# Batch 0's v issued by SyncE, q and k issued first by GpSimd

## The chip, the cores and the metric

The kernel runs on one core of a Trainium2 chip. The metric is device time in microseconds. Three runs of the kernel before took 262.04, 263.99 and 264.71 us; their median is 263.99.

## The reference

Sparse attention over 4 batches, 8 heads, 768 positions and a head size of 64, followed by a gated feed-forward layer over all 3072 tokens:

```python
k_sum = k.reshape(B, H, nb, block, D).max(axis=3)      # block = 32, nb = 24
v_sum = v.reshape(B, H, nb, block, D).mean(axis=3)
scores_l = scale * q @ k.T      # kept where |i - j| < 16, otherwise -1e9
scores_s = scale * q @ k_sum.T + log(block)
a = softmax(concat(scores_l, scores_s))
attn = a @ concat(v, v_sum)
h = x @ w_in                    # x: attn with the heads side by side, 3072 x 512
out = (h * clip(h + 3, 0, 6) / 6) @ w_out
```

Inputs and output are float32. The kernel computes in bfloat16 on the matrix engine.

## The kernel before

The heads are taken in pairs: p = 0 to 3, two heads of 64 making 128 partitions. For each batch and pair the kernel brings q and k into transposed form (`Tq`, `K`), computes the local scores in blocks of 64 keys by 94 queries (`Sl`), the scores against the block maxima (`Ss`), and the weighted sum with its denominator (`AV`). The result, for half a batch at a time (384 tokens, eight such tiles), goes through the first projection (`F1`, w_in) and the second (`F2`, w_out).

Batch 0 has its own beginning. Its v is read in float32 into the tile `vf` by `load_vf(p)`, with two transfers of 192 KB per pair, one per head: partition k holds row k of each of the 12 key blocks, so each piece that is contiguous in memory is a row of 64 numbers, 256 bytes. From `vf` come two things. `vcast` (L247) casts it into the block-diagonal bfloat16 tile `vbd`. `vsum0` (L256) sums blocks of 32 rows with four matmuls per pair; every second pair the sums are copied out and moved into the layout of `vst` by a small transfer that SyncE issues (L263). The loads of q and k (`load_q`, `load_k`) cast from float32 to bfloat16 on the way. They take pair 0, pair 1, and pairs 2 and 3 together; of q only the first 480 rows come at first, and the other 288 rows of all pairs later, with one transfer (L432).

All loads before the change are issued by GpSimd (queue POOL), in the order in which they are written. Between them GpSimd makes the constants: `ident` for transposing (L155 to 158), the local `mask` (L165 to 172) and `hm4` for the block sums (L180 to 186). Behind them come four loads for each of w_in and w_out. At most eight of POOL's transfers are under way in the trace before its next one waits for an old one to land. `pace` (L519) holds the loads of batch 1 back until the first projection of tile 0 has come to its twelfth slice.

For the start PE, ACT and DVE, too, run in the order in which the code is written, and it is this order that decides who waits for v:

```python
    v_first(0)          # vcast(0), vsum0(0)
    zero_rest()
    v_first(1)
    K(0, 0)
    Tq(0, 0, 0)
    v_first(2)
    S_first(0)
    v_first(3)
    K(0, 1)
    Tq(0, 1, 0)
    S_first(1)
```

Then follow `K(0, 2)`, `Tq(0, 2, 0)`, the first `Ss` and `AV`, pair 3, and the rest of the first half's `AV`. The first projection of tile 0 needs the `AV` of all four pairs. After the start a plan of slots (`at_slot`) places the work of attention between the projections' matmuls.

Transposition is by TensorE for batches below NPE, which is 4 (L25), and by a transposing transfer (`X`) otherwise; with four batches `X` is never reached.

Of the kernel before, what the change touches and what calls it, by code (L numbers as in the profile page):

```python
# [32 lines left out]
def kernel(  # L33
# [9 lines left out]
    nc = tc.nc  # L43
    B, H, S, _ = q.shape
    NP = H // 2
# [36 lines left out]
    kb_t, qb_t, vr_t, vf = {}, {}, {}, {}  # L82

    def load_k(b, p, n=1):

        if b < NLONG:
            t = ld.tile([RP, 2 * n, RUN, D], BF16, tag=f"kb{n}", name="kb", bufs=2)
            nc.gpsimd.dma_start(out=t[:], in_=k[b, 2 * p:2 * p + 2 * n].rearrange("h (p s) d -> p h s d", s=RUN))
        else:
            t = ld.tile([128, NT, 2, D], BF16, tag="kb", name="kb")  # L90
            load_natural(t, k, b, p)
        for i in range(n):
            kb_t[b, p + i] = t, i

    def load_q(b, p, n=1, part=None):

        if b < NLONG:
            lo, hi, r = cut(part)
            t = ld.tile([(hi - lo) // r, 2 * n, r, D], BF16, tag=f"qb{n}", name="qb", bufs=1 if n == 4 else 2)
            nc.gpsimd.dma_start(  # L100
                out=t[:], in_=q[b, 2 * p:2 * p + 2 * n, lo:hi].rearrange("h (p s) d -> p h s d", s=r))
        else:
            t = ld.tile([128, NT, 2, D], BF16, tag="qb", name="qb")
            load_natural(t, q, b, p)
        for i in range(n):
            qb_t[b, p + i, part] = t, i

    def cut(part):
        return {None: (0, S, RUN), 0: (0, QCUT, RUN), 1: (QCUT, S, RUN)}[part]

    def load_natural(t, src, b, p):
        for j in range(2):
            nc.gpsimd.dma_start(out=t[:, :, j], in_=src[b, 2 * p + j].rearrange("(s p) d -> p s d", p=128))  # L113
# [9 lines left out]
    def load_vf(p):  # L123

        if not vf:
            t = gp.tile([128, NP, NK, D], F32, tag="g", name="vf")
            vf.update({i: t[:, i] for i in range(NP)})
        for j in range(2):
            nc.gpsimd.dma_start(out=vf[p][64 * j:64 * j + 64],  # L129
                                in_=v[0, 2 * p + j].rearrange("(n k) d -> k n d", k=KB))  # L130

    def load_vrows(b, g):
# [9 lines left out]
    def load_w_in(c):  # L142
        w = d_ff // 4
        nc.gpsimd.dma_start(out=w_in_sb[:, :, c * w:(c + 1) * w], in_=w_in_v[:, :, c * w:(c + 1) * w])

    def load_w_out(c):
# [4 lines left out]
    ctx.enter_context(tc.manual_schedule(engines={ET.Pool}))  # L151
    start = tc.manual_schedule(engines={ET.PE, ET.Activation, ET.DVE})
    start.__enter__()
    load_vf(0)
    ident = const.tile([128, 128], BF16, tag="id", name="ident")  # L155
    nc.gpsimd.memset(ident[:], 1.0)
    nc.gpsimd.affine_select(out=ident[:], in_=ident[:], compare_op=ALU.is_equal, fill=0.0, base=0,
                            channel_multiplier=1, pattern=[[-1, 128]])
    load_vf(1)
    load_k(0, 0)  # L160
    load_q(0, 0, 1, 0)
    load_vf(2)


    mask = const.tile([128, WIN], BF16, tag="mask", name="mask")  # L165
    nc.gpsimd.memset(mask[:], 1.0)
    for j in range(2):
# [2 lines left out]
                                channel_multiplier=-1, pattern=[[1, WIN]])  # L170
        nc.gpsimd.affine_select(out=m, in_=m, compare_op=ALU.is_ge, fill=0.0, base=2 * HALO,
                                channel_multiplier=1, pattern=[[-1, WIN]])
    load_vf(3)
    load_k(0, 1)
    load_q(0, 1, 1, 0)
    load_k(0, 2, 2)
    load_q(0, 2, 2, 0)


    hm4 = const.tile([RS, 4, D], F32, tag="hm4", name="hm4")  # L180
# [30 lines left out]
    for p in range(2, NP):  # L211
        zero_off_diagonal(nc.vector, vbd[p])
    NK0 = 7
    load_w_in(0)

    def zero_rest():
        for p in range(NP):
# [356 lines left out]
```

## Time and profile before

| | |
|---|---|
| median of three runs | 263.99 us |
| profiled execution: its time / its span | 264.71 / 263.0 us |
| PE busy | 240.5 us, 91% of the span |
| DVE, ACT, POOL busy | 156.5, 167.8, 71.9 us |
| transferred | 25.80 MB, of which 19.14 in GpSimd's queue and 6.34 in SyncE's |
| v of batch 0, eight issues by POOL | 788 ns each (median), 3.7 us from issue to landing |
| k and q of batch 0, pair 0 | issued at 5.03 and 5.67 us |
| w_in, four issues by POOL | 15.47 to 19.17 us, 12.4 us to landing |
| w_out, four issues by POOL | 19.17 to 26.1 us, 18.3 us to landing |

The span is the time from the first to the last instruction, and the device time holds 1.7 us more. A share of busy time averages over the whole run. In the slices each digit is a fortieth of the span, 6.6 us. In the DMA views q0 is the queue of what GpSimd issues, and q1 that of what SyncE issues; sizes are those of the destination, so that a casting load reads twice what is shown.

### The profile page before, as it was taken

Reading aid. Unit: us, or ns where it says so; the run is one execution under the profiler, and the core shown is the slowest. Engines: PE = TensorE matmul, PEld = TensorE weight load, DVE = VectorE, ACT = ScalarE, POOL = GpSimd, SP = SyncE. Lnnn points to the kernel's source line nnn. Section 1 sums busy time; section 2 is a strip of 40 time slices with the busy share of each in tenths; the row PEclk is TensorE's granted clock in tenths of the full one; section 3 lists DMA queues with packets and bytes.
Section 4 is the critical chain, followed back from the end, with each engine's and each line's share of the span. In section 5 each row is a group of like instructions: output and inputs, shape, how many; then the busy total and the mean of one; then the engine's idle time right before and its main releaser. Section 6 shows DMA issues by size and latency. Waiting matters only on the chain.

```text
span 263.0 us, 4992 instructions
## 1 busy us (share of the span) xinstructions
PE 240.5 (91%) x1936; PEld 136.5 (52%) x1936; DVE 156.5 (60%) x362; ACT 167.8 (64%) x325; POOL 71.9 (27%) x104
## 2 busy tenths in 40 slices
PE   0957989999999979999959999999999999999993
PEld 0225656644455546666625556566655555555541
DVE  6494756633899567999774566668534544444400
ACT  7664679833787858997745567757766555555410
POOL 8993000756281402896710210000000000000000
PEclk9995699999999999999999999999999999999999
DMA  3999995599999912999990551001011111101122
GB/s 110 180 145 202 206 206 85 83 192 211 215 248 108 182 45 51 88 163 163 189 94 12 60 70 41 35 9 42 0 40 42 40 40 42 40 0 41 42 80 80
DMA packets 56951, 25.80 MB, mean 98 GB/s; under 512 B 45152, under 2 KB 52320, under 8 KB 56928
## 3 DMA queue, kind: packets, MB, share of 16 engines
q0 software_dynamic: 53264, 19.14, 63.5%
q1 hardware_dynamic: 3664, 6.34, 6.4%
q8 instruction: 15, 0.25, 0.4%
q14 instruction: 8, 0.07, 0.1%
HBM read 31.98 MB, written 6.29 MB: 146 GB/s over the span
## 4 chain that ended last, share of the span: by engine, by line
PE 61%; DMA 13%; POOL 10%; DVE 6%; ACT 5%; issue 3%; POOLq 0%; ACTq 0%
PE op L422 24%; PE hp L409 23%; DMA vr<-in_v_dram 8%; DMA qb<-in_q_dram 3%; POOL vf L129 2%; PE num L379 2%; DVE g L413 2%; PE sl L341 2%; POOL vbd L120 2%; DMA kb<-in_k_dram 2%; PE ss L351 2%; PE num L377 2%; POOL qb L113 2%; PE den L383 1%; POOL kb L113 1%
## 5 line engine op out<-in xcount | busy, mean ns | idle before, releaser
L409 PE MATMUL hp<-x,win 128*128 128x384 bf16 x512 | 104.7, 326 | 4.6 <-DVE g L413 3.2
L412 ACT ACTIVATE r<-hp,half_c 128x384 f32<-128x384 f32 x128 | 73.5, 580 | 47.5 <-PE hp L409 46.7
L422 PE MATMUL op<-wout,g 128*128 128x512 bf16 x384 | 101.0, 379 | 0.0
L413 DVE SCALAR_TENSOR_TENSOR g<-r,hp 128x384 bf16<-128x384 f32 x128 | 69.8, 552 | 46.1 <-ACT r L412 45.9
L409 PEld LDWEIGHTS <-win 128*128 128x128 bf16 x512 | 47.5, 98 | 38.8 <-issue 7.8
L422 PEld LDWEIGHTS <-g 128*128 128x128 bf16 x384 | 36.6, 98 | 32.5 <-issue 0.6
L397 DVE TENSOR_TENSOR x<-num,lg 128x384 bf16<-128x384 f32 x32 | 17.8, 555 | 25.2 <-ACT lg L396 23.9
L120 POOL DMA_DIRECT2D vbd<-in_v_dram x24 | 18.1, 771 | 38.0 <-PE num L379 32.5
L395 ACT ACTIVATE lg<-den 128x384 f32<-128x384 f32 x32 | 15.7, 491 | 17.8 <-PE den L390 9.2
L344 ACT ACTIVATE at<-sl 128x376 bf16<-128x376 f32 (+2 forms) x48 | 22.3, 487 | 3.6 <-PE sl L341 3.6
L426 ACT COPY ot<-op 128x512 f32<-128x512 f32 x24 | 13.8, 584 | 8.9 <-PE op L422 8.8
L345 DVE TENSOR_TENSOR at<-at,mask 128x376 bf16<-128x376 bf16 (+2 forms) x48 | 16.3, 351 | 3.6 <-ACT at L344 3.5
L396 ACT ACTIVATE lg<-lg 128x384 f32<-128x384 f32 x32 | 16.8, 526 | 0.8
L379 PEld LDWEIGHTS <-vbd 128*128 128x128 bf16 x224 | 13.2, 101 | 8.0 <-issue 4.6
L341 PEld LDWEIGHTS <-kbd 128*128 128x128 bf16 x192 | 12.1, 100 | 8.2 <-DVE kbd L302 2.3
L341 PE MATMUL sl<-qT,kbd 128*128 128x94 bf16 x192 | 14.8, 211 | 1.6 <-DVE kbd L302 1.5
L113 POOL DMA_DIRECT2D qb<-in_q_dram x16 | 13.5, 858 | 4.4 <-DMA vr<-in_v_dram 2.9
L379 PE MATMUL num<-at,vbd 128*128 128x94 bf16 (+2 forms) x224 | 14.4, 204 | 0.0
L256 PE MATMUL vps<-vf,ind 128*8 128x384 f32 x16 | 7.7, 627 | 7.0 <-DMA vf<-in_v_dram 6.4
L113 POOL DMA_DIRECT2D kb<-in_k_dram x16 | 13.4, 860 | 0.9 <-DMA kb<-in_k_dram 0.9
L377 PE MATMUL num<-asum,vst 96*128 96x384 bf16 x32 | 10.8, 337 | 2.4 <-DVE x L397 1.6
L386 PE MATMUL den<-at,obd 128*128 128x384 bf16 x32 | 11.1, 345 | 0.0
(82 smaller groups left out, 218.9 us busy)
## 6 DMA issues: line engine op xcount, KB each, us to landing
out_dram<-ot SPq DMA_DIRECT2D x24, 256.0 KB, 2.1
vr<-in_v_dram POOLq DMA_DIRECT2D x6, 768.0 KB, 8.7
vbd<-in_v_dram POOLq DMA_DIRECT2D x24, 96.0 KB, 4.5
win<-in_moe_w_in_dram POOLq DMA_DIRECT2D x4, 512.0 KB, 12.4
wout<-in_moe_w_out_dram POOLq DMA_DIRECT2D x4, 512.0 KB, 18.3
vf<-in_v_dram POOLq DMA_DIRECT2D x8, 192.0 KB, 3.7
kb<-in_k_dram POOLq DMA_DIRECT2D x16, 96.0 KB, 7.2
qb<-in_q_dram POOLq DMA_DIRECT2D x16, 96.0 KB, 6.8
```

What stands on the lines that cost most here:

```text
L113: nc.gpsimd.dma_start(out=t[:, :, j], in_=src[b, 2 * p + j].rearrange("(s p) d -> p s d", p=128))
L120: nc.gpsimd.dma_start(out=vall[rows, p, lo:hi, rows], in_=v[b, 2 * p + j].rearrange("(n k) d -> k n d", k=KB)[:, lo:hi])
L341: nc.tensor.matmul(sp[:, i * WIN:(i + 1) * WIN], kbd[p][:, t], qT[p][:, PAD - HALO + t * KB:PAD - HALO + t * KB + WIN], start=True, stop=True)
L344: nc.scalar.activation(a, sp[:, 0:n * WIN].rearrange("p (n c) -> p n c", c=WIN), AF.Exp, scale=scl)
L345: nc.vector.tensor_tensor(a, a, mask[:].unsqueeze(1).to_broadcast([128, n, WIN]), op=ALU.mult)
L379: nc.tensor.matmul(num[:, lo:hi], vbd[p][:, t], a[:, t, off:off + hi - lo], start=False, stop=(i == len(bl) - 1))
L396: nc.scalar.activation(lg[:], lg[:], AF.Exp, scale=-1.0)
L397: nc.vector.tensor_tensor(xt[s][:, p], num[:], lg[:], op=ALU.mult)
L409: nc.tensor.matmul(hp[:], w_in_sb[:, kt, ft * 128:(ft + 1) * 128], xt[t][:, kt], start=(kt == 0), stop=(kt == NP - 1))
L412: nc.scalar.activation(r[:], hp[:], AF.Relu, bias=half_c[:], scale=1.0 / 6.0)
L413: nc.vector.scalar_tensor_tensor(gt[t][:, ft], r[:], 1.0, hp[:], op0=ALU.min, op1=ALU.mult)
L422: nc.tensor.matmul(op[:], gt[t][:, ft, ts * 128:(ts + 1) * 128], w_out_sb[:, ft], start=(ft == 0), stop=(ft == NFT - 1))
```

## The change

SyncE issues the loads of batch 0's v, all eight at the head of its program. GpSimd begins with k and q of pair 0, makes `ident`, and then issues k and q of the other pairs and the first quarter of w_in; `mask` and `hm4` come after these. The other loads keep their order. Nothing else in the program differs: what is computed, tiles, buffers and the order of PE, ACT and DVE are the same.

```diff
         for j in range(2):
-            nc.gpsimd.dma_start(out=vf[p][64 * j:64 * j + 64],
+            nc.sync.dma_start(out=vf[p][64 * j:64 * j + 64],
                                 in_=v[0, 2 * p + j].rearrange("(n k) d -> k n d", k=KB))
...
-    load_vf(0)
+    for p in range(NP):
+        load_vf(p)
+    load_k(0, 0)
+    load_q(0, 0, 1, 0)
     ident = const.tile([128, 128], BF16, tag="id", name="ident")
     nc.gpsimd.memset(ident[:], 1.0)
     nc.gpsimd.affine_select(out=ident[:], in_=ident[:], compare_op=ALU.is_equal, fill=0.0, base=0,
                             channel_multiplier=1, pattern=[[-1, 128]])
-    load_vf(1)
-    load_k(0, 0)
-    load_q(0, 0, 1, 0)
-    load_vf(2)
+    load_k(0, 1)
+    load_q(0, 1, 1, 0)
+    load_k(0, 2, 2)
+    load_q(0, 2, 2, 0)
+    load_w_in(0)
...
-    load_vf(3)
-    load_k(0, 1)
-    load_q(0, 1, 1, 0)
-    load_k(0, 2, 2)
-    load_q(0, 2, 2, 0)
...
     NK0 = 7
-    load_w_in(0)
```

The change was also announced as one in which TensorE transposes batch 3; the diff has nothing of it.

## The prediction

> **What bounds the kernel now.** I read the slices first, then the start of the instruction timeline, then the DMA view in short windows.
>
> ```profile
> PE   0957989999999979999959999999999999999993
> POOL 8993000756281402896710210000000000000000
> DMA  3999995599999912999990551001011111101122
> ```
>
> Forty slices of 6.6 us. From the third slice on PE is nearly full, so a saving must come from the first five, before the first projection is in its stride. There POOL is full (it issues every load of batch 0) and so are the DMA engines.
>
> ```profile
> 1.32 1.64 POOL L129 DMA_DIRECT2D vf<-in_v_dram  x2 [0.80 <-POOLq L558]
> ...
> 9.87 1.50 POOL L129 DMA_DIRECT2D vf<-in_v_dram  x2
> ...
> 14.48 1.45 PE L256 MATMUL vps<-vf,ind 128*8 128x384 f32 x4 [0.33 <-DMA vf<-in_v_dram]
> 15.86 0.40 PEld L293 LDWEIGHTS <-kb 96*64 96x64 bf16 x16 [0.65 <-DMA kb<-in_k_dram]
> 20.47 0.81 PE L293 MATMUL tp<-ident,kb 96*64 96x96 bf16 x16 [1.72 <-DMA kb<-in_k_dram]
> 21.64 0.64 PE L332 MATMUL tp<-ident,qb 60*64 60x60 bf16 x16 [0.36 <-DMA qb<-in_q_dram]
> ...
> 35.36 1.30 PE L409 MATMUL hp<-x,win 128*128 128x384 bf16 x7 [0.17 <-DVE x L397]
> ```
>
> Columns: start, time, what, idle before it with its releaser. PE works strictly in the written order: the block sums of v (pairs 0 and 1) stand ahead of the first k transpose, those of pair 3 ahead of K(0,1). The last v lands at 14.4. The projection flows at 35.36, which is 20.9 us later, and of these PE waited 1.72 + 0.36 = 2.1 us for k and q of pair 2. The chain of waits says the same: POOL's issues up to 13.3, 8.26 us of DMA for the last q, then PE, ACT and DVE in turn to 35.36. After that its order is fixed and batch 1's loads hang on the projection itself (the pace copy at 47.43), so what the start loses or wins goes through to the end.
>
> **How the DMA engines share.** Three windows of the DMA view: 35 to 42 us, 21.75 to 22.5 us, 2.9 to 6.4 us. After the queue's name: packets, MB, busy share.
>
> ```profile
> q0 software_dynamic: 1403, 1.39, 120.1%
> ...
> q0 software_dynamic: 138, 0.13, 108.5%
> q1 hardware_dynamic: 51, 0.01, 12.7%
> ...
> DMA packets 212, 0.67 MB, mean 192 GB/s; under 512 B 48, under 2 KB 48, under 8 KB 212
> ```
>
> First window: GpSimd's casting loads, 1024-byte packets, alone: 7.0 us x 16 engines / 1403 = 80 ns each. Second: SyncE's small sums (vs96) beside them. Their packets are single 256-byte rows, and vs96 leaves 8 completion packets of 4 bytes, so it runs on 8 engines: 0.75 us x 8 / 51 = 118 ns each. The packet records show one run starting at 21.453, 21.558, 21.663, 21.767, 21.872: a 256-byte packet every 105 ns, one for each 80 ns packet of the other queue plus 25 for itself. With nothing beside them such packets start every 14 ns (14.338, 14.352, 14.366). Third: v as GpSimd loads it now goes in 4096-byte packets (164 of the 212 are over 2 KB), 384 in all.
>
> **What the Trainium skill says**, all on its page "DMA: Bandwidth & Descriptors". "Queues, rings and completion order": an engine takes turns between rows of queues, a packet at a time. The 105 ns steps agree. "SWDGE vs HWDGE vs iDMA": a packet is preferably up to 4096 B, in its account of the software path; v's 4096-byte packets agree, and SyncE's rows here go out singly (256 B for vs96, 2048 B for the outputs). "Issuing engines are not separate DMA queues": a second issuer saves sequencer time only. "Latency and other measured facts": first byte some 0.6 us for SyncE against 1 us for GpSimd. The trace differs: first packets came 2.7 us (vs96) and 2.0 us (first output, 69.12 to 71.15) after SyncE's issue, 1.6 us after GpSimd's (1.32 to 2.92). The trace decides, so SyncE gets no head start.
>
> **The change, part by part.**
>
> 1. *POOL is relieved.* Eight issues of v at 788 ns, 6.3 us, leave it. k and q of pair 0 go out at 1.32 instead of 5.03; ident (0.6 us) ends near 3.6, long before its first use behind two pairs of v; k and q of pairs 1 and 2 are out by 6.2 (four at 0.67) instead of 14.0; w_in(0) at 6.2 instead of 15.47. The mask (1.75 us with gaps) ends near 8.7 instead of 9.9, first needed at 15.28; hm4 near 10.2, first needed at 19.92. Alone, this removes the 2.1 us of waits above and up to 1 us of those at 14.48 and 15.86: a gain of 2 to 3 us.
>
> 2. *v's packets.* 8 x 192 KB in 256-byte rows is 6144 packets, 384 for each of 16 engines, instead of 24 of 4096 bytes. The trace of before has no such load from memory, so I bound it. Lower bound: 14 ns each alone, 5.4 us for all. Upper, by the row of the contention: 105 ns each, 40 us. I take the upper, because GpSimd's queue is not empty: k and q of part 0 (1248 packets), w_in (2048), the rest of q (288) and w_out (2048) make 5632, 352 an engine, and POOL issues them with few pauses. Up to the mask it has handed out 110 packets an engine by 7 us, worth 110 x 105 ns = 11.5 us; the mask and hm4 pause it for 3.2 us only. Its waits for earlier landings come when four or more transfers are still queued.
>
> 3. *When v lands.* SyncE issues near 0.85, first packets near 3.0, the same moment as k's (1.32 + 1.6). 352 turns x 105 ns = 37.0, so 40.0; the last 32 alone, 0.5 to 1; landing 1.2 after the last packet, as now (13.1 to 14.4): 41.9. Small gaps in POOL's supply before 5.2 us, in which SyncE's packets run at 14 ns, take off about 1: **41 us for the last v** (pair 0 near 14, pair 1 near 24, pair 2 near 34) against 14.4.
>
> 4. *Who waits.* PE stands at vsum0(0), then vsum0(1), and K(0,0), Tq(0,0,0), S_first(0) queue behind though k, q and ident are there by 7; ACT and DVE stand at the casts L247 with zero_rest and the off-diagonal zeros behind. SP's own vs96 moves queue behind the remaining v in the same rings; their users (vst, L459 and after) come after the last v anyway. Weights landing at 41 to 43 instead of 43.5 help nobody: the projection starts later than that.
>
> 5. *Sum.* Last v 41 - 14.4 = 26.6 later, less the 2.1 us of waits that go: the projection starts 24.5 us later, near 60, and all behind it moves along. Span 263.0 + 24.5 = 287.5. The profiled execution took 264.71, so 289.2 on its own scale; the median 263.99 is 0.7 less: **288.5 us**.
>
> 6. *Batch 3.* The words promise a transposition by TensorE, but NPE is 4 already and the diff doesn't touch it. Cost nothing; that part is not there to be gained.
>
> Unknown sizes: a 256-byte read from memory may cost more in a turn than the 25 ns of vs96; at 128 ns a turn v lands near 49, 297 us. The TensorE clock of 0.53 between 20 and 28 us may or may not recur in the late start: 2 us either way, inside that.
>
> **The rivals.**
>
> *Not slower:* SyncE's descriptors of one partition row travel as one packet of 12 x 256 = 3072 bytes. Then v needs 32 turns an engine, each about 125 ns (3072/4096 of the 165 that the records of GpSimd's 4096-byte packets show) plus 80, 6.6 us in all: last v landed at 11, last q near 15. PE is then bound by its own work, and K(0,2) starts near 17.8 instead of 20.47: 2.7 us less, 261.3. For it: GpSimd's v is packed. Against: every SyncE packet in the trace is a single row, though vs96's source and the outputs' target are contiguous. It decides once the last v lands before 14.4 + 2.1 = 16.5, that is at 32 ns or less a 256-byte piece on average.
>
> *Half of it:* SyncE's queue gets two or three packets a turn. Two: 192 turns x 129 ns, landed at 29, +12.5, 276.5. Three: 128 x 154 ns, landed at 24, +7.4, 271.4. The steps of 105 ns speak against it; one output does show that a turn isn't always one record: its 128 packets had 1196 of 128 bytes beside them (133.4 to 137.0 us).
>
> *No change:* the DMA engines bound the start either way, and POOL's earlier issues buy just what v's smaller packets cost: 264. Against it: the engines' share was only 0.67 from 2.9 to 6.4.
>
> **How the numbers follow.** One packet a turn 0.70, half of it 0.12, packed rows 0.13, no change 0.05. The likeliest case alone spans 277 to 297. The packed case straddles the bound of 1%, about what a measurement of this kernel tells from no change, at 261.3: half faster, half the same; the no-change case is the same. Faster 0.07, same 0.11, slower 0.82. To leave out no more than 2 in 10 the range has to reach from the packed case to the top of the likeliest: 261 to 297.
>
> **What would show it.** Right: some 6144 packets of 256 bytes in the hardware queue between 3 and 41 us beside a full software queue; casts L247 waiting for vf, about 10 us from pair to pair; PE nearly idle before 40; K(0,1) straight behind the last v; from 60 on the same picture as now from 35. Wrong: hardware packets of 3072 bytes, or 256-byte ones closer than 100 ns beside the 1024-byte ones, or the first projection before 50.

## The result and the profile after

Slower, as forecast, by less than forecast: a median of 279.06 us (276.69 to 281.61) against 263.62, ratio 1.056 with an interval of 1.046 to 1.066. The forecast was 288.5 with a range of 261 to 297. One of the four runs was in a slower state (281.61); here and below the ratios are of runs outside it, against runs of the kernel before made alongside. The profiled execution took 276.69, with a span of 274.8.

The slices of the page after, with the TensorE clock that was granted:

```profile
PE   0713578899999997999999999999999999999994
...
PEclk9975557999999999999999999999999999999998
DMA  7999990007999969069999063110001001001111
```

Each slice is now 6.9 us. Before, PE was short of work behind the first slice in the third and fourth only, at 5 and 7 tenths; now the second to sixth slices, 7 to 41 us, stand at 7, 1, 3, 5 and 7 tenths, while the DMA engines are full throughout. The instruction timeline of PE says what it waits for:

```profile
11.51 1.45 PE L254 MATMUL vps<-vf,ind 128*8 128x384 f32 x4 [1.95 <-DMA vf<-in_v_dram]
12.89 0.53 PE L291 MATMUL tp<-ident,kb 96*64 96x96 bf16 x16
19.59 2.72 PE L254 MATMUL vps<-vf,ind 128*8 128x384 f32 x4 [5.81 <-DMA vf<-in_v_dram]
...
29.81 2.72 PE L254 MATMUL vps<-vf,ind 128*8 128x384 f32 x4 [6.84 <-DMA vf<-in_v_dram]
32.45 0.85 PE L291 MATMUL tp<-ident,kb 96*64 96x96 bf16 x16
35.85 0.85 PE L291 MATMUL tp<-ident,kb 96*64 96x96 bf16 x16
...
50.22 1.30 PE L407 MATMUL hp<-x,win 128*128 128x384 bf16 x7 [0.17 <-DVE x L395]
```

Every block sum of v waits for its transfer, the last until 29.7 us. The transposes of k that follow wait for nothing: k and q had landed. The projection flows at 50.22 instead of 35.36, 14.9 us later, and the hold on batch 1's loads falls at 62.28 instead of 47.43: the whole program has moved along.

How the two queues shared, from the DMA view: the page's total for SyncE's queue, and then the windows 3 to 11 us, 6 to 7 us and 12 to 24 us (packets, MB, and the busy share, in which packets that overlap are each counted in full):

```profile
q1 hardware_dynamic: 9936, 7.92, 9.8%
...
q0 software_dynamic: 857, 0.80, 67.6%
q1 hardware_dynamic: 3118, 0.78, 56.3%
...
q1 hardware_dynamic: 715, 0.18, 129.6%
q0 software_dynamic: 16, 0.01, 8.3%
...
q0 software_dynamic: 1997, 1.85, 91.2%
q1 hardware_dynamic: 1997, 0.50, 30.7%
```

SyncE's queue has 6272 packets more than before: 6144 of 256 bytes and 16 completions for each of eight transfers. From 12 to 24 us both queues moved 1997 packets, one for one, though GpSimd's carried almost four times the bytes: 12.0 us x 16 / 1997 = 96 ns a turn. But before that, between 3 and 11 us, SyncE's queue moved 3118 against 857.

The span grew by 11.8 us only, 3 less than the projection's delay. The two profiles show where the rest went. In the execution profiled before, VectorE waited 3.5 us at 130 to 133 for rows of batch 3's v, whose transfer took 10.2 us from issue to landing, and PE waited for VectorE. In the profile after, the three such transfers between 100 and 160 us took 6.5 to 7.3, and PE has no gap there. First the kernel before, then after, the same matmuls:

```profile
134.35 0.81 PE L409 MATMUL hp<-x,win 128*128 128x384 bf16 x4 [2.24 <-DVE g L413]
136.49 0.81 PE L409 MATMUL hp<-x,win 128*128 128x384 bf16 x4 [0.35 <-DVE g L413]
```

```profile
146.72 0.81 PE L407 MATMUL hp<-x,win 128*128 128x384 bf16 x4
148.34 0.81 PE L407 MATMUL hp<-x,win 128*128 128x384 bf16 x4
```

So the two profiled executions, the slowest of before and the fastest of after, understate the change. The ratio of 1.056 is 14.8 us, close to the projection's 14.9.

### The profile page after: what moved, and what is told of

Same layout as the page of the kernel before. It is cut to its first block, busy times and chain, and to the rows that moved or that the text cites. A ratio compares the mean times of both kernels' runs of the same rounds, so it can differ in the third digit from the quotient of the medians.

```text
span 274.8 us, 4999 instructions
## 1 busy us (share of the span) xinstructions
PE 242.4 (88%) x1936; PEld 137.2 (50%) x1936; DVE 156.3 (57%) x362; ACT 167.6 (61%) x325; POOL 65.6 (24%) x96
## 4 chain that ended last, share of the span: by engine, by line
PE 60%; DMA 18%; DVE 7%; ACT 5%; POOL 3%; SPq 3%; issue 2%; ACTq 0%; POOLq 0%
PE op L420 23%; PE hp L407 22%; DMA vf<-in_v_dram 8%; DMA vr<-in_v_dram 7%; DMA kb<-in_k_dram 4%; SPq L129 3%; PE num L377 2%; DVE g L411 2%; PE sl L339 2%; POOL vbd L120 2%; PE num L375 2%; PE ss L349 1%; PE den L381 1%; PE den L384 1%; PE tp L330 1%
## 5 line engine op out<-in xcount | busy, mean ns | idle before, releaser
L395 DVE TENSOR_TENSOR x<-num,lg 128x384 bf16<-128x384 f32 x32 | 17.8, 555 | 24.6 <-ACT lg L394 23.3
L342 ACT ACTIVATE at<-sl 128x376 bf16<-128x376 f32 (+2 forms) x48 | 22.3, 486 | 10.4 <-PE sl L339 10.4
L254 PE MATMUL vps<-vf,ind 128*8 128x384 f32 x16 | 9.6, 746 | 21.4 <-DMA vf<-in_v_dram 21.4
L393 ACT ACTIVATE lg<-den 128x384 f32<-128x384 f32 x32 | 15.7, 490 | 17.8 <-PE den L388 9.2
L113 POOL DMA_DIRECT2D qb<-in_q_dram x16 | 13.5, 859 | 5.3 <-DMA vr<-in_v_dram 5.3
L254 PEld LDWEIGHTS vps<-vf,ind 128*8 128x8 f32 x16 | 1.5, 105 | 26.5 <-issue 26.0
L113 POOL DMA_DIRECT2D kb<-in_k_dram x16 | 13.4, 858 | 0.1
```

What stands on the lines that cost most here:

```text
L342: nc.scalar.activation(a, sp[:, 0:n * WIN].rearrange("p (n c) -> p n c", c=WIN), AF.Exp, scale=scl)
L395: nc.vector.tensor_tensor(xt[s][:, p], num[:], lg[:], op=ALU.mult)
```

## The experiments

The theory under test, called that of turns: as long as GpSimd's queue has packets ready, each 256-byte packet of SyncE waits for one of them, whatever the size of either. Its rivals: SyncE's own issue of so many short rows is slow (issuer; its eight issues lasted until 13.7 us); and the moved loads of k, q and w_in do the harm (order).

### Each half of the change alone

`e1_sync_only`: SyncE issues v; POOL's order is that of before.

```diff
-            nc.gpsimd.dma_start(out=vf[p][64 * j:64 * j + 64],
+            nc.sync.dma_start(out=vf[p][64 * j:64 * j + 64],
```

> SyncE issues v, GpSimd keeps the order of before without it. Turns theory (a 256-byte packet of SyncE's queue waits for one casting packet of GpSimd's queue): GpSimd's queue still fills up with q, k and the weights by 9 us, only some 3 us later than in the changed kernel, so the last v lands at 26 to 29 us and the time is 275 to 279. Order theory (what hurts is that k, q and w_in were moved ahead): 264 or less. Issuer theory (SyncE's own issue of 256-byte rows is slow, whatever else moves): as the changed kernel, 279.

Measured: 275.87 us, ratio 1.046 (1.040 to 1.052). The cast of the last v and the projection:

```profile
28.47 0.56 DVE L247 CAST vbd<-vf 64x768 bf16<-64x768 f32 x1 [4.10 <-DMA vf<-in_v_dram]
...
48.43 1.30 PE L409 MATMUL hp<-x,win 128*128 128x384 bf16 x7 [0.17 <-DVE x L397]
```

`e2_order_only`: the changed kernel with `nc.gpsimd` in that line.

> GpSimd issues v, all eight first, then k and q and the rest in the changed order. Turns theory: v travels in 4096-byte packets and lands by 10 us, k and q of pair 0 land 1 to 2 us later than before, pairs 2 and 3 a little earlier: 262 to 266. Order theory: near 279. Issuer theory: 262 to 266.

Measured: 265.63 us, ratio 1.007 (1.004 to 1.010).

The harm comes with the issuing queue: with it alone the projection is 13.1 us late, of the 14.9. The order alone costs 0.7%; k of pair 0 is issued at 7.78 us there, behind the eight issues of v, instead of at 5.03.

### The weights kept out of the way

`e3_hold_weights`: two copies on GpSimd that read the last v stand ahead of w_in.

```diff
-    load_w_in(0)
...
+    for j in range(2):
+        nc.gpsimd.tensor_copy(hold[64 * j:64 * j + 1], vf[3][64 * j:64 * j + 1, 0, 0:2])
+    load_w_in(0)
```

> The changed kernel, but GpSimd waits for the last v before it issues w_in, the rest of q and w_out (mask and hm4 are made before that). Turns theory: only k and q (78 packets an engine) stand against v, so the last v lands at 12 to 15 us and the first projection flows at 32 to 35: 260 to 265, faster than before if anything. Issuer theory: v lands near 28 as in the changed kernel and the weights come later still: 279 or more. Order theory: 264, since w_in is back behind.

Measured: 266.86 us, ratio 1.012 (1.009 to 1.016).

```profile
18.66 1.45 PE L257 MATMUL vps<-vf,ind 128*8 128x384 f32 x4
...
36.75 1.30 PE L410 MATMUL hp<-x,win 128*128 128x384 bf16 x7 [0.17 <-DVE x L398]
```

The last v landed near 18.5, not 12 to 15, the projection flowed at 36.75, not 32 to 35, and the time is above the expected 260 to 265. Of the projection's delay 13.5 us are gone all the same, so it is GpSimd's filled queue that holds v up, and not SyncE's issue. The expected times were too early because I had counted SyncE's packets at 14 ns when alone; the next run shows what they take.

### SyncE's queue alone

`e6_hold_all`: the same two copies ahead of all of GpSimd's loads.

> The changed kernel, but GpSimd waits for the last v before it issues anything, so SyncE's queue is alone. Turns theory: 384 packets an engine at 15 to 18 ns each after 2.4 us: last v at 8 to 10.5 us, and the time is 263 to 267, since k and q only start then. Issuer theory: the last v lands at 20 us or later, 280 or more.

Measured: 265.91 us, ratio 1.015 (1.009 to 1.021). The DMA view from 2.4 to 10.4 us:

```profile
q1 hardware_dynamic: 5900, 1.48, 130.7%
```

8.0 us x 16 / 5900 = 22 ns a packet: read from memory and alone, such rows take 22 ns instead of the 14 of vs96, and v is there at 12.1, later than the expected 8 to 10.5. All 384 packets an engine need some 8.5 us. The same with e3: 78 turns x 96 + 306 x 22 = 14.2 us, from 2.4 on 16.6, and the landing. The issuer theory is out: alone, SyncE's eight issues are over at 7.5 us instead of 13.7; beside k and q only, in e3, they still lasted until 13.4. So it is traffic of GpSimd's that stretches them.

### The same bytes in fewer packets, and in longer turns

`e4_long_rows` gives each partition 12 consecutive rows of v instead of every 64th: the same bytes in pieces of 3072. The rest of the kernel expects the rows as they were, so the result is another one.

```diff
-                                in_=v[0, 2 * p + j].rearrange("(n k) d -> k n d", k=KB))
+                                in_=v[0, 2 * p + j].rearrange("(k n) d -> k n d", k=KB))
```

> The changed kernel with v of batch 0 read so that a partition gets 12 consecutive rows (3072 bytes in one piece) instead of every 64th row; same bytes, the rows are permuted, so the result differs. Turns theory: 32 packets an engine instead of 384, last v by 10 to 13 us, 259 to 264. Issuer theory, if it is the count of pieces that SyncE is slow in: the same. Order theory: near 279. If the number of bytes, not of packets, is what counts: near 279.

Measured: 261.54 us, ratio 0.989 (0.979 to 0.999). SyncE's packets have 3072 bytes, 32 an engine, and the last v landed at 13.6 us. PE's timeline shows K(0,0), K(0,1) and K(0,2) without a wait:

```profile
10.75 0.53 PE L291 MATMUL tp<-ident,kb 96*64 96x96 bf16 x16
15.14 0.53 PE L291 MATMUL tp<-ident,kb 96*64 96x96 bf16 x16
...
18.21 0.53 PE L291 MATMUL tp<-ident,kb 96*64 96x96 bf16 x16
```

`e7_long_weights` goes the other way: w_in is read in rows of the full width, so that its packets have 4096 bytes instead of 1024.

```diff
-        w = d_ff // 4
-        nc.gpsimd.dma_start(out=w_in_sb[:, :, c * w:(c + 1) * w], in_=w_in_v[:, :, c * w:(c + 1) * w])
+        nc.gpsimd.dma_start(out=w_in_sb[:, c], in_=w_in_v[:, c])
```

> The changed kernel with w_in read by rows of the full width: 4096-byte packets in GpSimd's queue instead of 1024, same bytes. Turns theory: a turn beside w_in lasts some 336 ns instead of 96, so v gets 32 turns in the time of 128; the last v lands at 35 to 37 instead of 29.7 and the time is 284 to 288. Issuer theory, and a theory in which the queues share by bytes: no change, 279.

Measured: 286.86 us, ratio 1.092 (1.087 to 1.096); the last v landed at 38.4. The DMA view from 16 to 24 us:

```profile
q0 software_dynamic: 723, 1.47, 94.8%
q1 hardware_dynamic: 724, 0.18, 15.9%
```

Again one for one, now at 8.0 x 16 / 724 = 177 ns a turn, with GpSimd's mean packet twice as long: half of its data packets in this window still have 1024 bytes. From 16 to 18 us, where all have 4096, 111 packets went against 111, 288 ns a turn and not the expected 336; the landing came later than the expected 35 to 37 all the same. v lands 8.7 us later for a change to w_in that leaves its bytes as they are. That excludes a sharing by bytes and the issuer theory, which both expected no change.

### Part of v by SyncE

`e5_half`: one head of each pair by SyncE, the other by GpSimd ahead of k and q.

```diff
+            (nc.gpsimd if j else nc.sync).dma_start(out=vf[p][64 * j:64 * j + 64],
```

> The changed kernel with one head of each pair of v issued by SyncE and the other by GpSimd, ahead of k and q. Turns theory: 192 packets an engine in SyncE's queue; in the changed kernel 225 an engine were through by 11 us, so v lands by 10 to 12, k of pair 0 by 8: 261 to 265. Issuer theory: half the pieces, v lands near 15 to 18, 264 to 268.

Measured: 265.86 us, ratio 1.014 (1.008 to 1.021). The time is just outside the range of the turns and inside that of the issuer, but v is not: all of it had landed by 12.0, as the turns have it, and not at 15 to 18. What is late is k of pair 0, landed at 12.9 and not by 8: it is issued at 4.42 behind four loads of v and shares the engines with the rest of it.

```profile
12.95 0.85 PE L291 MATMUL tp<-ident,kb 96*64 96x96 bf16 x16 [3.09 <-DMA kb<-in_k_dram]
```

`e8_first_pair` leaves to SyncE only what GpSimd's queue can't yet fill, pair 0. `e9_reorder` is the same order with pair 0 issued by GpSimd.

```diff
-    load_vf(0)
+    load_vf(0, nc.sync)
+    load_k(0, 0)
+    load_q(0, 0, 1, 0)
+    load_vf(1, nc.gpsimd)
     ident = const.tile([128, 128], BF16, tag="id", name="ident")
...
+    load_vf(2, nc.gpsimd)
+    load_k(0, 1)
+    load_q(0, 1, 1, 0)
+    load_vf(3, nc.gpsimd)
+    load_k(0, 2, 2)
+    load_q(0, 2, 2, 0)
```

> A version meant to win: SyncE issues only pair 0 of v (96 packets an engine), GpSimd goes k and q of pair 0, v of pair 1, ident, v of pair 2, k and q of pair 1, v of pair 3, k and q of pairs 2 and 3, then mask, hm4 and the weights. Turns theory: SyncE's queue has only k and q of pair 0 (20 packets an engine) against it, 96 x 21 + 20 x 75 ns: pair 0 lands near 6.5, the last v near 12 to 13, the last q 2 to 3 us earlier than the 21.6 of before; the first projection flows 2 to 3 us earlier: 260.5 to 262 beside a before of 262.7, ratio 0.990 to 0.998. Issuer theory: pair 0 lands near 6.7 as in the changed kernel; no difference from this. If nothing is won, the start is bound by PE's own work.

> The same order, but pair 0 of v issued by GpSimd too, so that only the constants are moved behind the loads. POOL's issues are 1.6 us later than with SyncE's help, mask and hm4 3 us later than before: last q about 1 to 1.5 us earlier than before, 261.5 to 263.5, ratio 0.995 to 1.003.

Measured: e8 261.47 us, ratio 0.994 (0.990 to 0.997), so 0.6% faster than before; e9 262.17, ratio 0.998 (0.995 to 1.001). In e8 all of PE's waits for k and q are gone. What remains of waiting for v stands at its beginning, pair 0 (7.51 instead of 6.08 before), and at pair 3:

```profile
7.51 4.45 PE L256 MATMUL vps<-vf,ind 128*8 128x384 f32 x8 [7.51 <-DMA vf<-in_v_dram]
15.88 1.45 PE L256 MATMUL vps<-vf,ind 128*8 128x384 f32 x4 [1.11 <-DMA vf<-in_v_dram]
```

The projection flows at 33.98, 1.4 us earlier than before. That is less than the expected 2 to 3 us: pair 0 came at 7.4, not 6.5, and the last v at 15.8, not 12 to 13, which PE waited for. The intervals of e8 and e9 overlap, so what SyncE's one pair brings over the order alone isn't settled.

## Why the prediction was right, and where its size was off

1. *POOL relieved:* as said. k of pair 0 at 1.35, the last q issued at 5.31, w_in(0) at 5.96, mask and hm4 ready by 9.8. k and q had landed before PE asked, and the wait of 1.72 us at K(0,2) is gone.

2. *v's packets:* the count, 6144, was exact. Beside a full queue the upper bound was right: a turn took 96 ns instead of 105. The lower bound of 14 ns was too low: 22 alone.

3. *When v lands:* here the size was lost, since far fewer than the 352 turns an engine took place. Two terms failed. The first is "SyncE gets no head start": SyncE's packets began at 2.36 us and GpSimd's at 3.07, and 631 of SyncE's, 39 an engine, went before that. The second, and larger, is "small gaps in POOL's supply before 5.2 us take off about 1". At 105 ns a turn, 76 packets an engine would have gone from 3 to 11 us; the records show 3054 of 256 bytes, 191 an engine. POOL had handed out its 110 packets an engine by 7, just as predicted, but of these only 777 packets of 1024 bytes, 49 an engine, had started by 11. Turns with what did start, and SyncE's other packets alone, fill this stretch: 857 / 16 x 96 ns + (3118 - 857) / 16 x 22 ns = 8.25 us, in a window of 8. By then 225 an engine of v's 384 were through. The remaining 159 did take turns: 159 x 96 ns = 15.3, on average over at 26.3; the slowest engines and the landing bring it to 29.7, 11.3 us earlier than the 41 forecast. So there were some 210 turns an engine, about 50 before 11 us and 159 after. The pairs came at 6.7, 11.4, 19.5 and 29.7 instead of 14, 24, 34 and 41: the step of 10 us is there between the last two, in which the turns rule.

4. *Who waits:* as said. PE waited 21.4 us for v, and the rest stood behind. Pair 0's k was transposed at 12.89, straight after the second pair's sums.

5. *The sum:* 2.1 us of waits were to come off behind the last v; the net was 0.4, for 29.7 to 50.22 is 20.5 us and it was 20.9. From K(0,1) to the projection it is 17.8 instead of 19.5, so most of the 2.1 came off there. But between the last v and K(0,1) it took 2.75 us instead of 1.4: the four sums took 2.72 instead of 1.45 us, as did those of pair 2, while those of pair 1, behind a wait of 1.95 us only, took 1.45. The windows of after, 14 to 20, 20 to 28 and 28 to 43 us (the columns are the times, busy PE, PEld, DVE, ACT and POOL, then the granted clock, DMA share and GB/s):

```profile
14.00:20.00 6.00, 0.41 (x1) 0.12 (x2) 2.71 (x5) 1.54 (x3) 2.07 (x3) 0.75 1.22 196
20.00:28.00 8.00, 2.97 (x11) 0.79 (x9) 0.61 (x3) 1.61 (x3) 0.00 (x0) 0.50 1.22 197
28.00:43.00 15.00, 11.29 (x136) 6.98 (x137) 7.95 (x17) 6.77 (x14) 0.00 (x0) 0.50 0.95 157
```

   The clock falls to 0.50 while PE stands and waits for v. The Trainium skill, "TensorE: Matmul & The Clock Gate", section "Part 1: The HAM clock gate (the "warmup" mystery)", says that half the clock is the state of an idle matrix engine and that activity releases it. The first two windows agree with the first half. The second half isn't plain here: the clock stayed at 0.50 from 28 to 43 us, in which PE was busy for 11.3 of 15, and before the change it was 0.53 from 20 to 28 us with PE busy for 6.6 of 8. No run was made on the cause. What is shown is the slow work just behind the last wait, some 1.3 us: the prediction's 2 us either way came out on the slow side. With 11.3 us less at v and 1.7 less saved, 24.5 becomes 14.9.

6. *The rivals:* packed rows were to gain 2.7 us, with v landed at 11 (261.3). When e4 brought them about they gained 1.1%, 3.0 us, with v landed at 13.6 and no wait of PE for it. SyncE's queue doesn't pack rows of 256 bytes by itself. "Half of it" had the landing almost right, 29 with two packets a turn, and its 276.5 is nearer to the 279.06 than the 288.5. But where the queue of GpSimd was full, one packet went a turn, not two; that the average over the whole load comes out near two (384 packets in some 210 turns) comes from the stretch before 11 us, in which few of GpSimd's packets had started. As a forecast of the time it would have been right by luck.

7. *The signs:* the 6144 packets, the waiting casts and K(0,1) straight behind the last v are there. But so is, strictly taken, one of the signs of being wrong, packets closer than 100 ns beside the 1024-byte ones (96 in the full stretch, far closer before 11 us), and the projection at 50.22 just missed another, "before 50". Direction and mechanism were right; how long the mechanism ruled was not.

The Trainium skill's statement on turns, "DMA: Bandwidth & Descriptors", section "Queues, rings and completion order", is what carried the forecast, and 1997 against 1997 agrees with it. Its section "Issuing engines are not separate DMA queues" says that a second issuer only saves sequencer time; here it also changed the packets, and with them v's share of the engines, and the measurement decides: 1.046 for e1, in which nothing but the issuer of v differs.

## What to carry to other kernels

Before a load is moved to another issuing queue, count its packets and ask how full the other queue is while it runs: beside a full queue its time is packets an engine times one packet of each queue, not bytes over bandwidth. Short rows belong in the queue in which they are packed, as GpSimd's was here, or into a stretch in which the other queue has little, as pair 0 in e8. And ask when the other queue's packets start, not when they are issued: that was most of the 11 us by which v came before its forecast. Where an engine works in written order, the load at the head of that order decides, so freeing the issuing engine is worth only what the head of the order gains.

## What the runs showed of the hardware

- GpSimd's packets started late beside a dense stream from SyncE. k of pair 1, issued at 3.31, had its first packets at 6.9 us, 3.6 us after the issue against 1.7 for the first load; k and q of pair 0 stood ahead of it in the queue until 6.6. From 6 to 7 us GpSimd's queue moved 16 packets against 715. In e1 the same k, issued at 4.41, had its first packets at 8.2, with nothing left ahead of it since 6.8: from 7 to 8 us there are 612 packets of SyncE's queue and none of GpSimd's. In e4, with 3072-byte packets in SyncE's queue, there is no such gap. Why the queue starts so slowly isn't settled; no run was made for it.
- SyncE's first packet came 1.55 us after its first issue (0.81 to 2.36), not the 2.0 to 2.7 that later issues showed before.
- A 256-byte row that SyncE loads takes 22 ns of an engine alone (e6). One such row and one 1024-byte packet of GpSimd take 96 ns together, one row and a 4096-byte packet 288 (e7, 16 to 18 us).
